# Reordering vector sums, weight splits and loads in a one-core adaLN attention and gated MLP kernel

## The chip, the cores and the metric

The kernel runs on one core of one Trainium2 chip. The metric is the device time of one execution in microseconds (us). An engine is called by its name in the profile: PE (TensorE matmuls), PEld (its weight loads), DVE (VectorE), ACT (ScalarE), POOL (GpSimd), SP (the engine that issues most loads). Each of them takes its instructions strictly in the order in which the program wrote them.

## The reference

What is computed is a transformer block on 2048 tokens of width 576, in float32:

```python
mod = silu(c) @ w_mod                         # six rows sa, ca, ga, sb, cb, gb
h = layernorm(x) * (1 + ca) + sa
q = (h @ wq) as 32 heads of 128;  k, v = last 512 cached keys, 16 heads, each used by 2 query heads
o = softmax(q @ k.T * 128 ** -0.5) @ v
x = x + ga * (o @ wo)
h = layernorm(x) * (1 + cb) + sb
x = x + gb * ((relu(h @ W_gate) * (h @ W_up)) @ W_down)     # inner width 4608
```

## The kernel before, in words

**Precision.** Matmul operands are pairs: a rounded high part (`hi`) and the rest, the low part (`lo` = value - hi). A product takes three matmuls: hi·hi, lo·hi, hi·lo. The high part is a copy on ACT, the low part a subtraction on POOL (`split`, L175 to 177, for weights).

**Attention.** The work is cut into 128 *units*. A unit is one query head and one block of 512 queries, against 512 keys. Units 0 to 87 go through KV heads 0 to 10 with all four query blocks (8 units a head). Units 88 to 107 do heads 11 to 15 for query blocks 0 and 1, units 108 to 127 the same heads for blocks 2 and 3, with 4 units a head. In unit u, PE does in this order: scores (`s_half`, 12 matmuls of 128x512), the query projection for unit u+1 (`qproj`, 14 matmuls), one small matmul that sends maxima and sums across partitions (`spread`, tile `qm`, L474), a quarter of an output projection (`piece`, 12 matmuls of 128x288), half of the product with the values of unit u-1 (`pv_half`, 6 matmuls), the other half, and a second quarter of an output projection.

The vector work of unit u hangs on this chain. DVE takes the maxima of the two score halves (L451), prepares them (L459, L460), sums the probabilities of unit u-1 over the partitions (`sum_pre`, L466, which reads `ks`), and then PE can do `spread`. After it DVE transposes the maxima (L489, L479, L504), subtracts them from the scores (L521, two instructions), and ACT does the exponentials (L523) and the high parts `hi` (L510). Then follow on DVE: `sum_bc` (L484, tile `rb`), `q_lo` (L430, the low part of the next queries), the first half of the probability sum (`ksum_op(u, 0)`, L536, which reads the first half of the exponentials), and `o_mul` (L556). POOL makes the low parts `lo` of the probabilities (`lo_half`, L530, one instruction for each half), the second half of the probability sum (`ksum_op(u, 1)`, L539, two instructions) and the low part of an attention output (`o_lo`, L564). In the program POOL's order is `lo` half 0, the sum, `lo` half 1. ACT also copies the output projection's PSUM result into `acc` (L584) and, where the next quarter allows it, puts `acc` into PSUM ahead of that quarter as a seed (L608).

**The order of side work** is written out by hand: `step(name, t, fn)` queues a function at time t, where unit u covers t = 10u to 10u + 9, and `run(u, k)` issues what is due at ten places in a unit. Place 0 lies ahead of the scores, 1 behind them, 2 behind the projection, 4 ahead of the exponentials, 5 between the two exponentials, 6 and 7 behind them, 8 ahead of `hi` of half 1, and 9 behind everything. Side work of this kind is:

- Weights for the next head (`prep`, `weights`, L1125): a load into one of two `raw` buffers on SP, for the output weights a multiplication with the gate row on DVE (*gate*, L217, tile `roga`), and a split on ACT and POOL (L176, L177). `gap` says how many quarter-units ahead of the split the load is written. "Parked" weights (`parks`) of heads 12 to 15 are prepared early and kept in HBM.
- `lay` (L1183): copies in HBM that bring the MLP weights into another layout, one every half unit, units 12 to 79, on SP.
- `prep_mod`: rows of `w_mod`, loads on SP and one multiply-add on DVE each (L128), every five units from unit 10.
- `w_later` (L823): the first MLP step needs seven combinations of weight blocks (`WTERMS`: P1, P2, P4 have one term, P7 and P5 two, P6 three, P3 four), in two halves each, 14 items in all. An item loads its terms from HBM, adds them on POOL (`comb`, L840), rounds on ACT (L849), subtracts on POOL (L850, L852) and stores both parts to HBM. The stores go out on ACT's queue (`flush_stores`). Before, they run in units 26 to 87, in `wp` weight buffers (tile `wx`).
- Behind unit 107 the second layer norm of blocks 0 and 1 (`norm_steps("b0")`, `("b1")`): statistics, normalising on ACT (`nm`), transposes on PE through the single PSUM buffer `psW` (`tr`, tile `ltb`, L317), scale and shift on ACT and DVE (`af`), stores. Then `h0_load`, `h0_cut`, `h0_comb` make the combined inputs of the MLP's first step.

**MLP.** 36 steps of seven products each (2 halves of the tokens, 18 blocks of the inner width), PE nearly alone at the end.

Of the kernel before, what the change touches and what calls it, by code (L numbers as in the profile page):

```python
# [7 lines left out]
F32 = mybir.dt.float32  # L8
F32R = mybir.dt.float32r
# [5 lines left out]
P = 128  # L15
# [18 lines left out]
def kernel(  # L34
# [614 lines left out]
    dkeep = [dr.tile([P, 2, D], F32R, name=f"dk{f}") for f in range(NFT)]  # L649
    stores = []  # L650

    def flush_stores():
        while stores:
            dst, src = stores.pop(0)
            nc.scalar.dma_start(dst.bitcast(F32), src.bitcast(F32))

# [163 lines left out]
    WTERMS = {"P1": "+00", "P2": "+01", "P6": "+10+11-00", "P7": "+00-10", "P5": "+10+11", "P4": "+11",  # L820
              "P3": "+01-10-11+00"}

    def w_later(s, xx, tag):  # L823
        st = {}
        eng = nc.gpsimd
        terms = terms_of(s, WTERMS)

        def get(dst, i, j):
            nc.sync.dma_start(dst, wlay[i, j, :, xx, :])

        def begin():
            w = wp.tile([P, 1280], F32, tag=tag, name=f"wx_{s}_{xx}")
            for k, x in enumerate("abh"):
                st[x] = w[:, 384 * k:384 * k + 384]
            for x, term in zip("ab", terms):
                get(st[x], *term[1:])

        def comb(i):
            x, y = st["a"], st["b"]
            eng.tensor_tensor(x, x, y, op=ALU.add if terms[i][0] == "+" else ALU.subtract)  # L840
            if i + 1 < len(terms):
                get(st["b"], *terms[i + 1][1:])
            else:
                cut()

        def cut():
            a = st["a"]
            hi = st["h"].bitcast(F32R)
            nc.scalar.copy(hi, a)  # L849
            nc.gpsimd.tensor_sub(hi[0:32, 256:], a[0:32, 256:], hi[0:32, 256:].bitcast(F32))  # L850
            lo = st["b"][:, :256].bitcast(F32R)
            nc.gpsimd.tensor_sub(lo, a[:, :256], hi[:, :256].bitcast(F32))  # L852
            stores.append((wkeep[0, s][:, xx, 0:3, :].rearrange("p t n -> p (t n)"), hi))
            stores.append((wkeep[0, s][:, xx, 3:5, :].rearrange("p t n -> p (t n)"), lo))

        return [begin] + ([cut] if len(terms) == 1 else [lambda i=i: comb(i) for i in range(1, len(terms))])
# [241 lines left out]
    for t in range(5):  # L1098
# [8 lines left out]
               (49, 46, 49), (("m", "aav", "vvv"), ("w", "vvv", "vvv"), ("w", "aav")))  # L1107
    H = 10 * UNITS.index((HKV - 1, 1, HQ - 1))
    norm_steps("b0", 0, "b", None, None, (H + 16, H + 20, H + 26, H + 29), H + 30,
               (H + 34, H + 36, H + 44, H + 46), (H + 48, H + 58, H + 68), (H + 49, H + 59, H + 69), www)  # L1110
    norm_steps("b1", 1, "b", None, None, (H + 34, H + 37, H + 40, H + 47), H + 48,
               (H + 54, H + 56, H + 64, H + 66), (H + 78, H + 88, H + 98), (H + 79, H + 89, H + 99), www)
    po = prep_out(wos, 0, wo, "ga")
    step("wo0.l", 19, po[0])
    step("wo0.g", 20, po[1])
# [9 lines left out]
    def weights(g, d):  # L1125

        h = 2 * g
        return [(("q", h), d["q"], prep5(d["q"], h, wq, "wA")), (("k", g), d["k"], prep_kv(d["k"], g, 0)),
                (("q", h + 1), d["q"], prep5(d["q"], h + 1, wq, "wA")),
                (("v", g), d["v"], prep_kv(d["v"], g, 1)), (("o", h), d["o"], prep_out(d["o"], h, wo, "ga")),  # L1130
                (("o", h + 1), d["o"], prep_out(d["o"], h + 1, wo, "ga"))]
# [6 lines left out]
    for i in range(1, len(VIS)):  # L1138
        g, qbs = VIS[i]
        B = 10 * UNITS.index((g, qbs[0], 2 * g))  # L1140
        if g in early or g in seen:
            for key, t in zip((("q", 2 * g), ("k", g), ("q", 2 * g + 1), ("v", g), ("o", 2 * g),
                               ("o", 2 * g + 1)), (-30, -20, -14, 0) + ((-4, -4) if i > first + 1 else (6, 34))):
                step("again", B + t, again, key, live[key[0]], key[1],
                     key[0] == "o" and key[1] % 2 and i > first and (i - first) % 2 == 0)
        else:
            for (key, d, pr), t in zip(weights(g, live), (-30, -20, -14, 0, 20, 34)):
                prep(key[0] + str(key[1]), B + t, pr, 3)
                if any(v[0] == g for v in VIS[i + 1:]):
                    sk(B + t + 12, key, d, key[1])  # L1150
        seen.add(g)
    WL = {i: [] for i in range(1, first)}
    longs = [(s, xx) for s in ("P3", "P6") for xx in range(2)]
    shorts = [(s, xx) for s in ("P1", "P2", "P7", "P5", "P4") for xx in range(2)]
    for i in range(1, first):
        B = 80 * i
        for c, t in (("q", 10), ("kv", 26), ("o", 44)):
            if parks[c]:
                key, d, pr = parks[c].pop(0)
                prep("park", B + t, pr, 3)  # L1160
                sk(B + t + 9, key, d, key[1])
        todo = []
        if i > 2:
            if longs or shorts:
                todo.append(((longs or shorts).pop(0), "wA", (24, 30, 36, 40)))
            if shorts:
                todo.append((shorts.pop(0), "wB", (40, 46)))
        for (s, xx), tag, ts in todo:
            fns = w_later(s, xx, tag)
            for fn, t in zip(fns, ts):  # L1170
                step("w.l", B + t, fn)
            step("w.st", B + ts[len(fns) - 1] + 5, flush_stores)
    assert not any(parks.values()) and not longs and not shorts
    for i in range(15):
        prep(f"m{3 + i // 5}.{i % 5}", 104 + 50 * i, prep_mod(3 + i // 5, i % 5))
    step("m3.col", 310, setd(mods, "b0", lambda: mod_col(3, 0.0)()))
# [71 lines left out]

    def then(fn):
        def go():  # L1250
            flush_stores()
            fn()
        return go

    t0 = H + 70
    for t in range(3):
        step("h0.l", t0, h0_load, 0, 0, t)
        step("h0.l", t0, h0_load, 1, 0, t)
    cuts = [("B11", (0, 0), t) for t in range(3)] + [("B21", (1, 0), t) for t in range(3)]
    for n, c in enumerate(cuts):  # L1260
        step("h0.c", t0 + 4 + 4 * n, then(lambda c=c: h0_cut(*c)))
    t0 = H + 100
    seq = []
    for t in range(3):
        step("h0.l", t0 + 4 * t, h0_load, 1, 1, t)
# [43 lines left out]
    run(-1, 9)  # L1309
    for u in range(NU):  # L1310
        run(u, 0)
        if u > 1:
            o_hi(u - 2)
            o_lo(u - 2)
        s_half(u, 0)
        s_half(u, 1)
        max_pre(u)
        if u:
            sum_pre(u - 1)
        run(u, 1)  # L1320
        if u + 1 < NU:
            qproj(u + 1, 0, 14)
        run(u, 2)
        spread(u)
        max_bc(u)
        if u + 1 < NU:
            q_hi(u + 1)
        run(u, 3)
        if 10 * u + 3 in at:
            piece(at[10 * u + 3])  # L1330
        run(u, 4)
        if u:
            pv_half(u - 1, 0)
        flush(pend_act)
        exp_half(u, 0)
        flush()
        run(u, 5)
        exp_half(u, 1)
        lo_half(u, 0)
        if u:  # L1340
            sum_bc(u - 1)
        if u + 1 < NU:
            q_lo(u + 1)
        run(u, 6)
        if u:
            pv_half(u - 1, 1)
        if 10 * u + 6 in at:
            piece(at[10 * u + 6])
        ksum_op(u, 0)
        run(u, 7)  # L1350
        if u:
            o_mul(u - 1)
        flush()
        run(u, 8)
        hi_half(u, 1)
        flush(pend_act)
        ksum_op(u, 1)
        lo_half(u, 1)
        run(u, 9)
    for u in range(NU, NU + 8):  # L1360
# [55 lines left out]
```

## Time and profile before

| what | value |
|---|---|
| runs | 3150.45, 3148.22, 3150.13 us; median 3150.13 |
| profiled execution | 3152.37 us, of which 3150.3 us lie between its first and last instruction (the span) |
| PE busy | 2939.7 us, 93% of the span |
| DVE, ACT, POOL busy | 2131.5, 1361.2 and 1859.4 us |
| mean granted TensorE clock | 0.982 |
| attention (scores from 35.1 to 1760.1 us) | PE waits here and there, all engines busy |
| MLP after it | the same code in both kernels |

In the rows of the profile, `out<-in` names what an instruction writes and reads, without buffer numbers. "Idle before" is the time in which the engine had nothing running ahead of that instruction, with the engine or transfer that ended it.

### The profile page before, as it was taken

How to read it: one execution, taken by the hardware profiler on the slowest of the kernel's cores; microseconds unless marked ns; L12 is line 12 of the kernel's file. 1: busy time of each engine (PE TensorE's matmuls, PEld its weight loads, DVE VectorE, ACT ScalarE, POOL GpSimd, SP SyncE). 2: the span in 40 equal slices, each digit the busy share in tenths (PEclk: the TensorE clock that was granted, in tenths of full speed). 3: DMA queues.
4: the chain of work that ended last, by engine and by line, in shares of the span. 5: the costliest groups of instructions: out<-in, count | busy, mean ns of one | idle time of the engine just before them, and what ended most of it. 6: DMA issues, size and time to landing. Idle time of an engine off the chain costs nothing. (4 is left out here: it accounts for less than half of the span.)

```text
span 3150.3 us, 41269 instructions
## 1 busy us (share of the span) xinstructions
PE 2939.7 (93%) x15414; PEld 2535.5 (80%) x15414; DVE 2131.5 (68%) x2925; ACT 1361.2 (43%) x1885; POOL 1859.4 (59%) x1294
## 2 busy tenths in 40 slices
PE   6799989988999999999888989999999999999999
PEld 5688877877887888888777777878778888888888
DVE  7888877777878887778778555556667544444444
ACT  5566655655666666665555333232323211111110
POOL 5688877787888777767678555556666411111111
PEclk9999999999999999999999999999999999999999
DMA  3122122223223112212244465556777954444453
GB/s 142 31 63 67 64 99 93 100 91 105 80 78 108 36 36 72 91 69 80 86 166 152 159 217 194 209 200 231 263 268 254 335 184 171 164 164 157 167 175 112
DMA packets 173447, 435.82 MB, mean 138 GB/s; under 512 B 16128, under 2 KB 62976, under 8 KB 173248
## 3 DMA queue, kind: packets, MB, share of 16 engines
q1 hardware_dynamic: 131344, 291.36, 28.1%
q10 hardware_dynamic: 41904, 141.84, 11.6%
q8 instruction: 122, 2.00, 0.3%
q14 instruction: 77, 0.63, 0.1%
HBM read 283.71 MB, written 177.73 MB: 146 GB/s over the span
## 5 line engine op out<-in xcount | busy, mean ns | idle before, releaser
L530 POOL TENSOR_TENSOR lo<-p,hi 128x1024 fp32r<-128x1024 f32 x256 | 623.2, 2435 | 314.4 <-ACT hi L510 281.1
L575 PE MATMUL md<-wogb,hhi 128*128 128x288 f32 x2304 | 480.7, 301 | 52.7 <-ACT lflh L900 32.1
L915 PE MATMUL gu<-hop_T,wop 128*128 128x512 f32 (+1 forms) x2016 | 502.4, 394 | 1.2 <-DMA wop<-wk_P 1.2
L586 DVE TENSOR_TENSOR acc<-md,acc 128x576 f32<-128x576 f32 x288 | 217.4, 755 | 422.3 <-PE md L575 422.3
L575 PEld LDWEIGHTS md<-wogb,hhi 128*128 128x128 f32 x2304 | 392.5, 192 | 83.4 <-ACT lflh L900 37.3
L915 PEld LDWEIGHTS gu<-hop_T,wop 128*128 128x128 f32 (+1 forms) x2016 | 370.6, 189 | 69.8 <-DMA wop<-wk_P 1.6
L451 DVE TRANSPOSE_TENSOR_REDUCE t<-s 128x32 f32<-128x1024 f32 x256 | 314.0, 1239 | 131.7 <-PE s L448 122.3
L915 PE MATMUL gu<-hop_B,wop 128*128 128x512 f32 (+1 forms) x1512 | 380.3, 394 | 4.1 <-DMA wop<-wk_P 2.7
L539 POOL TENSOR_TENSOR ks<-ks,p 128x512 f32<-128x512 f32 x256 | 341.3, 1333 | 18.9 <-DVE ks L536 6.5
L575 PE MATMUL md<-wogb,hlo 128*128 128x288 f32 x1152 | 345.8, 300 | 2.3 <-POOL hlo L931 2.3
L931 POOL TENSOR_TENSOR hlo<-r,hhi 128x512 fp32r<-128x512 f32 x72 | 98.7, 1371 | 409.2 <-issue 242.3
L915 PEld LDWEIGHTS gu<-hop_B,wop 128*128 128x128 f32 (+1 forms) x1512 | 280.6, 190 | 60.6 <-DMA wop<-wk_P 3.2
L374 PE MATMUL qps<-hTa,wA 128*128 128x512 f32 x1288 | 311.8, 393 | 8.7 <-ACT lfa L356 4.9
L575 PE MATMUL wo<-woga,ohi 128*128 128x288 f32 x1472 | 313.6, 306 | 5.0 <-ACT wo L608 3.5
L374 PEld LDWEIGHTS qps<-hTa,wA 128*128 128x128 f32 x1288 | 244.1, 190 | 61.8 <-ACT lfa L356 5.3
L521 DVE TENSOR_TENSOR p<-s,mb 128x1024 f32<-128x1024 f32 x242 | 285.5, 1217 | 3.5
L510 ACT CAST hi<-p 128x1024 fp32r<-128x1024 f32 x256 | 269.1, 1051 | 6.8
L523 ACT ACTIVATE p<-p 128x1024 f32<-128x1024 f32 x242 | 255.7, 1056 | 16.9 <-DVE p L521 10.5
L575 PEld LDWEIGHTS wo<-woga,ohi 128*128 128x128 f32 x1472 | 244.0, 193 | 15.4 <-ACT wo L608 5.2
L930 ACT CAST hhi<-r 128x512 fp32r<-128x512 f32 x72 | 44.7, 621 | 432.7 <-DVE r L940 379.5
L575 PEld LDWEIGHTS md<-wogb,hlo 128*128 128x128 f32 x1152 | 221.8, 193 | 3.0 <-POOL hlo L931 3.0
L575 PE MATMUL wo<-woga,olo 128*128 128x288 f32 x736 | 220.3, 299 | 0.0
(198 smaller groups left out, 5803.0 us busy)
## 6 DMA issues: line engine op xcount, KB each, us to landing
wop<-wk_P SPq DMA_DIRECT2D x133, 640.0 KB
wk_P<-wop ACTq DMA_DIRECT2D x119, 640.0 KB
wr<-wlay SPq DMA_DIRECT2D x68, 384.0 KB
dk<-wogb ACTq DMA_DIRECT2D x36, 576.0 KB
wogb<-dk SPq DMA_DIRECT2D x36, 576.0 KB
againq<-akq SPq DMA_DIRECT2D x18, 640.0 KB
rogb<-wd SPq DMA_DIRECT2D x36, 288.0 KB
rwA<-wq SPq DMA_DIRECT2D x32, 320.0 KB
```

Source lines behind the costliest of these rows:

```text
L374: return [lambda i=i, a=a, b=b: nc.tensor.matmul(ps, a, b, start=(i == 0), stop=(i == n - 1)) for i, (a, b) in enumerate(ops)]
L451: nc.vector.tensor_reduce(t4[u][:, 2 * h:2 * h + 2, :].rearrange("p k b -> p (k b)"), t.rearrange("p k (b j) -> p (k b) j", j=32), axis=AX ...
L510: nc.scalar.copy(hi_[u, h], pt[u, h])
L521: nc.vector.tensor_tensor(p, t, bc[u][:, None, :].to_broadcast([P, 2, 512]), op=ALU.subtract)
L523: nc.scalar.activation(p, p, AF.Exp, bias=0.0, scale=1.0)
L530: nc.gpsimd.tensor_sub(lo_[u, h], pt[u, h], hi_[u, h].bitcast(F32))
L539: nc.gpsimd.tensor_tensor(ks_[u], ks_[u], p[:, j, :], op=ALU.add)
L575: nc.tensor.matmul(ps[:, half, :H2], a[:, sl], w[b][:, cs], start=(n == 0 and seed is None), stop=(n == 5), skip_group_check=seed is not None)
L586: nc.vector.tensor_tensor(av, ps[:, :, :H2], av, op=ALU.add)
L915: nc.tensor.matmul(ps, a, c, start=s not in ("P2", "P3") and i == 0, stop=i == len(ops) - 1, skip_group_check=True)
L930: nc.scalar.copy(hi, r)
L931: nc.gpsimd.tensor_sub(lo, r, hi.bitcast(F32))
```

## The change

It has five parts, all in the order of the program; no arithmetic is changed. Where the diff writes `H`, it is 1070.

1. **Probability sums first.** `ksum_op(u, 0)` and `ksum_op(u, 1)` are written directly behind the second exponential, ahead of both `lo_half` calls. On POOL the sum now stands ahead of both low parts; on DVE L536 stands ahead of `sum_bc` and `q_lo`.
2. **Odd units' output split later.** `o_hi` and `o_lo` of odd units move from the start of the unit to behind `pv_half(u - 1, 0)`.
3. **Weight loads and splits spaced anew.** `gap` 3 becomes 4 (6 for the last), the first output weights' split moves from place 20 to 10 of a head's 80, the parked ones from 10, 26, 44 to 16, 24, 44 with gaps 5, 5, 6.
4. **`w_later` moved and rebuilt.** All 14 items go from units 26 to 87 to t = 952 to 1142 (units 95 to 115). They use two small tiles `wa`, `wb` (the high part overwrites `wb`, the low part `wa`) instead of one large one: the first seven items in `xm` buffers (three of them, shared with `ks`), the others in `hT` buffers, which are free once unit 107's projection is done. `flush_stores(2)` in the second group and in `h0_cut`'s steps leaves the two newest stores for a later call.
5. **Second norm of blocks 0 and 1.** Transposes go from place 8 of a unit to place 1 of the next but two (`H + 48` to `H + 51`), that is behind the scores, the normalising from places 4 and 6 to place 9, and the `h0` steps go four places later.

```diff
-    def flush_stores():
-        while stores:
+    def flush_stores(left=0):
+        while len(stores) > left:
...
         def begin():
-            w = wp.tile([P, 1280], F32, tag=tag, name=f"wx_{s}_{xx}")
-            for k, x in enumerate("abh"):
-                st[x] = w[:, 384 * k:384 * k + 384]
+            for x in "ab":
+                st[x] = pool.tile([P, w], F32, tag=tag, name=f"w{x}_{s}_{xx}")[:, :384]
...
-            hi = st["h"].bitcast(F32R)
+            hi = st["b"].bitcast(F32R)
...
-            lo = st["b"][:, :256].bitcast(F32R)
+            lo = a[:, :256].bitcast(F32R)
...
     norm_steps("b0", 0, "b", None, None, (H + 16, H + 20, H + 26, H + 29), H + 30,
-               (H + 34, H + 36, H + 44, H + 46), (H + 48, H + 58, H + 68), (H + 49, H + 59, H + 69), www)
+               (H + 39, H + 39, H + 49, H + 49), (H + 51, H + 61, H + 71), (H + 51, H + 61, H + 71), www)
...
-            for (key, d, pr), t in zip(weights(g, live), (-30, -20, -14, 0, 20, 34)):
-                prep(key[0] + str(key[1]), B + t, pr, 3)
+            for (key, d, pr), t in zip(weights(g, live), (-30, -20, -14, 0, 10, 34)):
+                prep(key[0] + str(key[1]), B + t, pr, 6 if t == 34 else 4)
...
-        for c, t in (("q", 10), ("kv", 26), ("o", 44)):
-            if parks[c]:
+        for c, t, gap, a in (("q", 16, 5, 0), ("kv", 24, 5, 1), ("o", 44, 6, 2)):
+            if parks[c] and i > a:
...
-        if i > 2:
-            if longs or shorts:
-                todo.append(((longs or shorts).pop(0), "wA", (24, 30, 36, 40)))
-            if shorts:
-                todo.append((shorts.pop(0), "wB", (40, 46)))
...
+    t = 952
+    items = [(s, xx) for s in ("P1", "P2", "P4", "P7", "P5", "P6", "P3") for xx in range(2)]
+    for n, (s, xx) in enumerate(items):
+        here = n < 7
+        for fn in w_later(s, xx, (xp, "xm", 640) if here else (hp, "hT", 512)):
+            step("w.l", t, fn if here else then(fn))
+            t += 5 if here else 4
+        if here:
+            step("w.e", t + 3, flush_stores)
+            t = t + 5 if n < 6 else 1062
+    step("w.e", t + 6, flush_stores)
...
-        if u > 1:
+        if u > 1 and u % 2 == 0:
             o_hi(u - 2)
             o_lo(u - 2)
...
             pv_half(u - 1, 0)
+        if u > 1 and u % 2:
+            o_hi(u - 2)
+            o_lo(u - 2)
         flush(pend_act)
         exp_half(u, 0)
         flush()
         run(u, 5)
         exp_half(u, 1)
-        lo_half(u, 0)
+        ksum_op(u, 0)
+        ksum_op(u, 1)
         if u:
             sum_bc(u - 1)
...
-        ksum_op(u, 0)
...
-        ksum_op(u, 1)
+        lo_half(u, 0)
         lo_half(u, 1)
```

POOL in units 60 and 61, before (`ks` is the probability sum, `lo` a low part, `wx` a `w_later` item, `wA` and `kv` weight splits):

```order
L530 TENSOR_TENSOR lo_0_8432<-p_0_8424,hi_0_8427 128x1024
L840 TENSOR_TENSOR wx_P_1_8341<-wx_P_1_8341 128x384
L850 TENSOR_TENSOR wx_P_1_8341<-wx_P_1_8341 32x128
L852 TENSOR_TENSOR wx_P_1_8341<-wx_P_1_8341 128x256
L539 TENSOR_TENSOR ks_8461<-ks_8461,p_1_8429 128x512 x2
L530 TENSOR_TENSOR lo_1_8471<-p_1_8429,hi_1_8464 128x1024
L177 TENSOR_TENSOR wA_8473<-rwA_8407,wA_8473 128x640
L564 TENSOR_TENSOR olo_8479<-rb_8434,ohi_8477 128x512
```

The same place now:

```order
L539 TENSOR_TENSOR ks_8321<-ks_8321,p_1_8318 128x512 x2
L530 TENSOR_TENSOR lo_0_8354<-p_0_8313,hi_0_8316 128x1024
L530 TENSOR_TENSOR lo_1_8356<-p_1_8318,hi_1_8349 128x1024
L177 TENSOR_TENSOR wA_8358<-rwA_8232,wA_8358 128x640
L564 TENSOR_TENSOR olo_8433<-rb_8325,ohi_8431 128x512
```

The sum no longer stands behind a low part and, here, a `wx` item.

DVE in unit 61, before (`p` is the subtraction ahead of the exponential, `t` with scores behind it the next unit's maxima):

```order
L521 TENSOR_TENSOR p_0_8555<-s_0_8481,mb_8525 128x1024
L521 TENSOR_TENSOR p_1_8560<-s_1_8490,mb_8525 128x1024
L484 STREAM_TRANSPOSE rb_8565<-ri_8523 128x512
L430 SCALAR_TENSOR_TENSOR qlo_8567<-qps_8505,qhi_8527 128x512
L536 TENSOR_TENSOR ks_8588<-p_0_8555 128x512
L556 TENSOR_TENSOR rb_8565<-pv_8545,rb_8565 128x512
L451 TENSOR_REDUCE t_62_8617<-s_0_8610 128x32
```

The same place now:

```order
L521 TENSOR_TENSOR p_0_8438<-s_0_8364,mb_8406 128x1024
L521 TENSOR_TENSOR p_1_8443<-s_1_8373,mb_8406 128x1024
L536 TENSOR_TENSOR ks_8446<-p_0_8438 128x512
L484 STREAM_TRANSPOSE rb_8450<-ri_8404 128x512
L430 SCALAR_TENSOR_TENSOR qlo_8452<-qps_8386,qhi_8408 128x512
L556 TENSOR_TENSOR rb_8450<-pv_8424,rb_8450 128x512
L451 TENSOR_REDUCE t_62_8500<-s_0_8493 128x32
```

`ks` reads the finished exponential, and `rb` and `qlo` now stand behind it.

ACT from the second exponential of unit 106 to the first of unit 107, before:

```order
L523 ACTIVATE p_1_14079<-p_1_14079 128x1024
L510 CAST hi_1_14111<-p_1_14079 128x1024
L584 COPY acc_131<-wo_2_14072 128x576
L608 COPY wo_3_14114<-acc_132 128x2x288
L560 CAST ohi_14120<-rb_14084 128x512
L426 ACTIVATE qhi_14168<-qps_14146 128x512
L584 COPY acc_132<-wo_3_14114 128x576
L608 COPY wo_0_14190<-acc_125 128x2x288
L523 ACTIVATE p_0_14192<-p_0_14192 128x1024
```

The same place now (`wb` is the rounding copy of a `w_later` item, which waits for POOL's `comb`):

```order
L523 ACTIVATE p_1_14015<-p_1_14015 128x1024
L849 CAST wb_P_1_13976<-wa_P_1_13975 128x384
L510 CAST hi_1_14051<-p_1_14015 128x1024
L584 COPY acc_131<-wo_2_14008 128x576
L608 COPY wo_3_14054<-acc_132 128x2x288
L426 ACTIVATE qhi_14108<-qps_14086 128x512
L849 CAST wb_P_0_14061<-wa_P_0_14060 128x384
L560 CAST ohi_14133<-rb_14022 128x512
L584 COPY acc_132<-wo_3_14054 128x576
L608 COPY wo_0_14138<-acc_125 128x2x288
L523 ACTIVATE p_0_14140<-p_0_14140 128x1024
```

Two rounding copies have come in, one ahead of `hi` of half 1, one ahead of the next unit's first exponential, and `ohi` of the odd unit stands behind `qhi`.

More of the change, by code (lines that the diff above doesn't have):

```diff
@@ L821, with w_later @@
               "P3": "+01-10-11+00"}
-    def w_later(s, xx, tag):
+    def w_later(s, xx, where):
+        pool, tag, w = where
         st = {}
@@ L1109 @@
     norm_steps("b0", 0, "b", None, None, (H + 16, H + 20, H + 26, H + 29), H + 30,
-               (H + 34, H + 36, H + 44, H + 46), (H + 48, H + 58, H + 68), (H + 49, H + 59, H + 69), www)
+               (H + 39, H + 39, H + 49, H + 49), (H + 51, H + 61, H + 71), (H + 51, H + 61, H + 71), www)
     norm_steps("b1", 1, "b", None, None, (H + 34, H + 37, H + 40, H + 47), H + 48,
-               (H + 54, H + 56, H + 64, H + 66), (H + 78, H + 88, H + 98), (H + 79, H + 89, H + 99), www)
+               (H + 59, H + 59, H + 69, H + 69), (H + 81, H + 91, H + 101), (H + 81, H + 91, H + 101), www)
     po = prep_out(wos, 0, wo, "ga")
@@ L1151 @@
         seen.add(g)
-    WL = {i: [] for i in range(1, first)}
-    longs = [(s, xx) for s in ("P3", "P6") for xx in range(2)]
-    shorts = [(s, xx) for s in ("P1", "P2", "P7", "P5", "P4") for xx in range(2)]
     for i in range(1, first):
         B = 80 * i
-        for c, t in (("q", 10), ("kv", 26), ("o", 44)):
-            if parks[c]:
+        for c, t, gap, a in (("q", 16, 5, 0), ("kv", 24, 5, 1), ("o", 44, 6, 2)):
+            if parks[c] and i > a:
                 key, d, pr = parks[c].pop(0)
-                prep("park", B + t, pr, 3)
+                prep("park", B + t, pr, gap)
                 sk(B + t + 9, key, d, key[1])
-        todo = []
-        if i > 2:
-            if longs or shorts:
-                todo.append(((longs or shorts).pop(0), "wA", (24, 30, 36, 40)))
-            if shorts:
-                todo.append((shorts.pop(0), "wB", (40, 46)))
[L1168 to L1173, printed above, removed]
+    assert not any(parks.values())
     for i in range(15):
@@ L1250, in go @@
         def go():
-            flush_stores()
+            flush_stores(2)
             fn()
         return go
-    t0 = H + 70
+    t = 952
[9 more added lines that the diff above has]
+    step("w.e", t + 6, flush_stores)
+    t0 = H + 74
     for t in range(3):
@@ L1261 @@
         step("h0.c", t0 + 4 + 4 * n, then(lambda c=c: h0_cut(*c)))
-    t0 = H + 100
+    t0 = H + 104
     seq = []
```

## The prediction

> **What bounds the kernel now.** I read the stretches first, counting PE's `spread` matmuls (line L474, two records a unit) in each. The columns are the stretch in us, its length, PE busy and count, PEld the same, granted clock, DMA share, GB/s.
>
> ```profile
> 133.00:374.20 241.20, 7.46 (x38) 6.35 (x39) 0.99 0.19 60
> 374.20:1137.50 763.30, 24.41 (x112) 18.87 (x113) 0.97 0.26 86
> 1137.50:1323.50 186.00, 6.02 (x30) 5.04 (x31) 1.00 0.20 66
> 1323.50:1481.00 157.50, 4.51 (x26) 4.98 (x27) 1.00 0.22 76
> 1481.00:1618.00 137.00, 3.54 (x19) 3.19 (x20) 0.98 0.33 112
> 1618.00:1763.00 145.00, 4.37 (x20) 2.85 (x19) 0.99 0.51 170
> ```
>
> In the fourth stretch (units 95 to 107) 13 units take 157.5 us, 12.1 each: PE never waits there, and no side work runs. That is the floor of a unit. The others hold 19, 56, 15, 9 and 10 units and take 11.3, 85.7, 4.5, 28.1 and 24.0 us more than 12.1 a unit. So 125 of these 154 us lie where the change takes something away, most of it in units 24 to 79, where `w_later` runs now.
>
> Next, who PE waits for: first in 374 to 1137 us, then (three rows) in 1481 to 1618, then in 1618 to 1763. The columns are us in total, times, longest.
>
> ```profile
> PE qm L474 <- DVE t L466: 47.4, 30, 6.6
> PE ltb L317 <- ACT acc L584: 6.7, 6, 2.8
> PE wo L575 <- ACT wo L608: 6.5, 7, 1.6
> PE qm L474 <- DVE t L466: 3.3, 2, 2.4
> PE qm L474 <- DVE t L466: 9.2, 7, 3.6
> ```
>
> `spread` waits for the sum over partitions. What makes that late stands in DVE's groups of 133 to 1323 us:
>
> ```profile
> L217 DVE TENSOR_TENSOR roga<-roga,mrow 128x576 f32<-128x576 f32 x30 | 75.6, 2520 | 28.5 <-DMA roga<-wo 28.5
> L466 DVE TRANSPOSE_TENSOR_REDUCE t<-ks 128x16 f32<-128x512 f32 x90 | 63.7, 708 | 38.5 <-POOL ks L539 36.9
> L536 DVE TENSOR_TENSOR ks<-p 128x512 f32<-128x512 f32 x90 | 62.4, 693 | 14.5 <-ACT p L523 14.5
> L128 DVE SCALAR_TENSOR_TENSOR macc<-wm,sT,macc 128x576 f32<-128x576 f32 x12 | 20.8, 1735 | 1.9 <-DMA wm<-wmod 1.9
> ```
>
> There are two causes: POOL's half of the probability sum (36.9 us of waiting), and gates whose weights have not landed (28.5 us, five times). The long ones cost more than they last. This is one, the wait ahead of unit 28, with a matmul behind it and the same matmul in an undisturbed unit:
>
> ```profile
> 426.18 2.40 DVE L217 TENSOR_TENSOR roga<-roga,mrow 128x576 f32<-128x576 f32 x1 [6.33 <-DMA roga<-wo]
> 432.11 0.71 PE L474 MATMUL qm<-t,quad 128*128 128x80 f32 x2 [6.59 <-DVE t L466]
> 433.18 0.44 PE L575 MATMUL wo<-woga,olo 128*128 128x288 f32 x1
> 1366.35 0.30 PE L575 MATMUL wo<-againo,olo 128*128 128x288 f32 x1
> ```
>
> The wait is 6.59 us, and the matmul then takes 0.44 instead of 0.30 us; the stretch's granted clock is 0.97 and not 1.00. So 85.7 us of excess stand against 47.4 us of `spread` waits. [...]
>
> **The sum ahead of the low parts.** An undisturbed unit (spread at 1360.3 us): DVE, ACT, POOL, the first score matmul that needs `qlo`, and the first matmul that needs the second low part:
>
> ```profile
> 1361.72 2.35 DVE L521 TENSOR_TENSOR p<-s,mb 128x1024 f32<-128x1024 f32 x2
> 1363.99 0.70 DVE L484 STREAM_TRANSPOSE rb<-ri 128x512 f32<-128x512 f32 x1
> 1364.62 0.65 DVE L430 SCALAR_TENSOR_TENSOR qlo<-qps,qhi 128x512 fp32r<-128x512 f32 x1
> 1365.19 0.67 DVE L536 TENSOR_TENSOR ks<-p 128x512 f32<-128x512 f32 x1
> 1363.66 1.05 ACT L523 ACTIVATE p<-p 128x1024 f32<-128x1024 f32 x1
> 1365.70 1.06 ACT L523 ACTIVATE p<-p 128x1024 f32<-128x1024 f32 x1
> 1365.88 2.41 POOL L530 TENSOR_TENSOR lo<-p,hi 128x1024 fp32r<-128x1024 f32 x1 [3.02 <-ACT hi L510]
> 1368.24 2.67 POOL L539 TENSOR_TENSOR ks<-ks,p 128x512 f32<-128x512 f32 x2
> 1370.86 2.39 POOL L530 TENSOR_TENSOR lo<-p,hi 128x1024 fp32r<-128x1024 f32 x1
> 1366.94 0.40 PE L448 MATMUL s<-qlo,againk 128*128 128x512 f32 x1
> 1376.08 0.39 PE L550 MATMUL pv<-lo,againv 128*128 128x512 f32 x1
> ```
>
> POOL's sum now ends at 1370.91. Written first, it starts when the second exponential ends (1366.76) and is done at 1369.4, 1.5 us earlier. A weight split or a `wx` item in front of it then no longer reaches `spread`, so the 36.9 us of waiting go. What is late next is the low parts: they end at 1369.4 + 4.8 = 1374.2 instead of 1373.25. PE needs the second one at 1376.1 (last row), so this is hidden with 1.9 us to spare.
>
> On DVE the sum's first half now waits for the first exponential. It starts at 1364.7 (1363.66 + 1.05) where `rb` started at 1363.99. At the rows' spacing of 0.6 us `qlo` starts two places later, at 1365.9, and ends at 1366.6 instead of 1365.3; PE needs it at 1366.94. The cover is 0.3 us. It holds in a plain unit. It does not in a unit with a multiply-add of `w_mod` ahead of the exponentials (1.74 us): there `qlo` comes at about 1367.7 to 1368.3, and I put 1 us on each of 15 such units.
>
> Odd units' `ohi` no longer stands ahead of `qhi`; ACT's exponential comes no later by it, and I cost it at nothing, since the copy that follows waits for PE anyway.
>
> **Gates.** Whether a gate delays the score maxima behind it hangs on what POOL is doing: a gate, POOL's instruction beside it, and a gate with POOL idle:
>
> ```profile
> 189.16 2.94 DVE L217 TENSOR_TENSOR roga<-roga,mrow 128x576 f32<-128x576 f32 x1
> 189.08 2.41 POOL L530 TENSOR_TENSOR lo<-p,hi 128x1024 fp32r<-128x1024 f32 x1 [2.35 <-ACT hi L510]
> 82.57 0.74 DVE L217 TENSOR_TENSOR roga<-roga,mrow 128x576 f32<-128x576 f32 x1
> ```
>
> The gate ends at 192.1, 0.6 us behind the low part's end at 191.5. After the change it starts about 0.75 us later in its unit, but POOL is in one of the two short sum instructions (1.33 us each), so it ends no later than now: 0.2 us for each of 30. If it took 2.94 us all the same, each would cost 0.75 us more, 22 us in all; that is a rival below. [...]
>
> **Loads and `w_later` taken away, units 5 to 94.** The five late gates stand where an item of three or four terms begins in the same place as the weight load. Those loads go, and the weight loads are written up to a unit earlier, so I let the 28.5 us go. Of 85.7 us there remain 11 multiply-adds at 1 us, 21 gates at 0.2, some 3 us of other waits, and the two column sums, which the change leaves alone:
>
> ```profile
> L165 PE MATMUL mps<-ones,macc 128*128 128x1 f32 x20 | 3.6, 289 | 4.4 <-DVE macc L162 2.6 <-DVE qlo L430 1.8
> ```
>
> These are 8.0 us, so 26 remain and 60 are gained. Of 11.3 us in the first stretch 4.5 remain (three multiply-adds, gates), of 4.5 in the third 3. The sum is 60 + 7 + 1.5 = **68 us gained**.
>
> **`w_later` put back, units 95 to 115.** Its instructions, ACT's wait for POOL in all (us, times), and the longest of these:
>
> ```profile
> L840 POOL TENSOR_TENSOR wx_P<-wx_P x14: 1012/1016/1506, 414.5 to 990.5; 128x384 f32<-128x384 f32 x14
> L849 ACT CAST wx_P<-wx_P x14: 493/511/517, 429.5 to 1094.1; 128x384 fp32r<-128x384 f32 x14
> L850 POOL TENSOR_TENSOR wx_P<-wx_P x14: 445/451/455, 430.0 to 1095.6; 32x128 fp32r<-32x128 f32 x14
> L852 POOL TENSOR_TENSOR wx_P<-wx_P x14: 716/727/738, 430.5 to 1096.1; 128x256 fp32r<-128x256 f32 x14
> POOL wx_P L840: 37.0, 8
> 429.46 0.51 ACT L849 CAST wx_P<-wx_P 128x384 fp32r<-128x384 f32 x1 [6.60 <-POOL wx_P L840]
> ```
>
> POOL's work is 14 x (1.02 + 0.45 + 0.73) = 31 us over 20 units, 1.5 a unit beside the 7.5 of 12.1 us that low parts and sum take above, and would fit. The order is the trouble. A rounding copy waits for POOL's last `comb`, eight items have one, and now (37.0 us in 8, 4.6 each) most of these waits stand at the start of a unit, where ACT idles. In the new order those of P5, the first of P6 and the first of P3 stand ahead of a unit's exponential. POOL reaches `comb` only behind the low parts of the unit before (about 1.8 us behind spread) and its last term arrives only after the `comb` before it. I put the copy's end 2 to 5 us behind where the exponential begins now, and `qlo` and the seed late by as much: 4 + 3 + 6.5 + 3.5. The last P3 copy holds up `hi` and both low parts, 4, and the other three cost 1.5 each. That is **25.5 us given back**, between 0 (all hidden) and 8 x 6.6 = 53 (the last row for each). For the six one-term items, whose loads share buffers with `ks`, I add 1.5: **27 us**.
>
> **Norm and `h0`.** The transposes are now covered by the 12 score matmuls, and the seed behind them by the projection's 14. Of the 6.7 + 6.5 us of waits I let 9 go, because some stand ahead of the first transpose. The `h0` steps fall on other places of a unit, which I cost at nothing, 5 us either way; POOL's earlier sum takes 2 of the 9.2 us in units 117 to 126. **11 us gained.**
>
> The sum is 68 - 27 + 11 = 52 us. The profiled execution took 3152.4 us, so 3100.4; the median of the runs lies 2.2 us below it, so **3098 us**. The MLP's code is the same.
>
> **The rivals.**
>
> *More is given back* (chance 0.20). The eight items cost the full 53 us: 3098 + 27 = 3125, from 3117 to 3140. For it: POOL, ACT and SP are in order, so one late term stops all three. Against: the stretch starts with no wait at all.
>
> *Gates still wait 2.9 us* (0.08): 3098 + 22 = 3120.
>
> *The late loads stay* (0.05), since HBM copies on SP's queue are the cause and not the items: 28.5 us, some 2 us of slower matmuls behind each (an estimate from 85.7 against 47.4), and 6 us of other waits in these units, about 45 us: 3143. The change would then not do what its second part says, and the result is at the edge of no change.
>
> *More is gained* (0.13): items hidden (12 instead of 27) and the multiply-adds' 15 us too: 3098 - 15 - 13 = 3070.
>
> *Slower* (0.06): the 0.3 us of cover ahead of `qlo` is not there. If the first exponential ends 0.3 us later than in the unit shown, every unit loses; at 0.8 us in 120 units 96 us come back, 3194. For it: L536 waited 14.5 us for exponentials already where it stood two instructions later. Against: in the unit shown it had 0.3 us to spare.
>
> **The numbers.** The forecast, 3075 to 3117, has 0.48. About 0.2% (6.3 us) is what a measurement of this kernel can tell from no change. Faster by more than that takes in the forecast, the first, second and fourth rival and part of the third: 0.89; within it 0.05; slower 0.06. The range from 3066 to 3130 leaves out the slower case, the late loads, and the ends of the two wide rivals, 2 in 10.
>
> **What would show it.** In the changed profile units 24 to 79 should take about 703 us, 12.6 each, at granted clock 1.00, with L466's wait for POOL gone and no row of L217 waiting for a load. Beside L448 a wait for `qlo` should stand only in units with a multiply-add. ACT's `wb` copy should wait for POOL in units 104 to 113 by 25 to 40 us, with PE waiting for `qlo` and for seeds there. The `ltb` waits should be gone. I am wrong if units 24 to 79 still take over 13 us, or if units 95 to 103, which lose nothing by my account, take over 12.3.

## The result, and the profile after

The changed kernel takes 3130.53 us (median of 4 runs, 3127.97 to 3133.55) against 3149.18 us for the kernel before in the same comparison: a ratio of 0.9944, 95% interval 0.9927 to 0.9961. It is faster, by 18.6 us, where 52 were forecast. The profiled execution took 3133.55 us, with a span of 3131.8.

These are the prediction's six stretches, cut at the same units. The columns are the stretch, its length, PE's `spread` matmuls (busy and count), granted clock, DMA share, GB/s.

```profile
143.00:379.50 236.50, 6.84 (x39) 1.00 0.16 50
379.50:1108.70 729.20, 20.27 (x112) 0.97 0.24 79
1108.70:1293.20 184.50, 5.36 (x30) 1.00 0.22 73
1293.20:1456.90 163.70, 4.51 (x26) 0.99 0.33 110
1456.90:1600.40 143.50, 3.64 (x19) 0.93 0.39 130
1600.40:1748.50 148.10, 4.09 (x20) 0.95 0.49 160
```

| part of the span | forecast, us | measured, us |
|---|---|---|
| up to unit 5 | 0 | +10.0 |
| units 5 to 23 | -7 | -4.7 |
| units 24 to 79 | -60 | -34.1 |
| units 80 to 94 | -1.5 | -1.5 |
| units 95 to 126 | -11 + 27 | +15.8 |
| behind unit 126 (MLP) | 0 | -4.0 |

So 26 us are missing in units 24 to 79, and 10 at the start, a stretch for which the prediction has no term. Units 24 to 79 take 13.02 us each at a granted clock of 0.97, where 12.6 at 1.00 were expected and more than 13 was named as the sign of being wrong. The last row is the spread between executions: the MLP's code is the same in all kernels of this study, and that part took 1381 to 1389 us in their profiles.

DVE's waits in units 24 to 79 (total, times, longest) say what kind of wait is left:

```profile
DVE macc L128 <- DMA wm<-wmod: 17.8, 3, 6.8
DVE macc L126 <- DMA wm<-wmod: 6.5, 1, 6.5
DVE roga L217 <- DMA roga<-wo: 0.9, 1, 0.9
```

The gates (28.5 us before) now have their weights, and L466's wait for POOL is gone, as forecast. But four multiply-adds of `prep_mod` wait for their row of `w_mod`. Before, one did, for 1.9 us. This is the one in unit 30: SP's queue, DVE, and some of PE's next score matmuls (start, duration):

```profile
449.70 0.58 SPq L1169 DMA_DIRECT2D wlay<-wu  x1
450.33 5.47 SPq L136 DMA_DIRECT2D wm<-wmod  x1
455.85 6.05 SPq L1169 DMA_DIRECT2D wlay<-wg  x2
461.83 0.82 DVE L128 SCALAR_TENSOR_TENSOR macc<-wm,sT,macc 128x576 f32<-128x576 f32 x1 [6.83 <-DMA wm<-wmod]
469.64 0.63 PE L447 MATMUL s<-qhi,kv 128*128 128x512 f32 x1
470.07 0.63 PE L448 MATMUL s<-qlo,kv 128*128 128x512 f32 x1
472.90 0.40 PE L446 MATMUL s<-qhi,kv 128*128 128x512 f32 x1
473.13 0.39 PE L447 MATMUL s<-qhi,kv 128*128 128x512 f32 x1
```

The load's issue, right behind an HBM copy, takes 5.47 us, and the row lands 6 us behind its end. Units 30, 35, 45 and 50, where these four waits stand, take 23.1, 20.7, 19.2 and 19.4 us: 82.4 together.

Behind unit 95 the profile is for the most part the forecast's (window 1293 to 1600 us):

```profile
ACT wb_P L849 <- POOL wa_P L840: 39.4, 8, 7.2
PE wo L575 <- ACT wo L608: 14.4, 10, 4.1
PE ltb L317 <- ACT acc L584: 2.1, 1, 2.1
```

ACT's rounding copies wait 39.4 us for POOL (25 to 40 forecast), PE pays with waits for seeds, though hardly for `qlo` (0.6 us), and `ltb`'s waits have shrunk from 6.7 to 2.1 us, where the forecast had them gone.

At the start, the stretch from 35 us to unit 5's `spread`, before and then after, and PE's new wait in it (all columns PE, PEld, DVE, ACT, POOL, clock, DMA share, GB/s):

```profile
35.00:132.90 97.90, 72.91 (x314) 56.29 (x312) 83.87 (x137) 47.73 (x68) 58.29 (x40) 0.91 0.09 31
```

```profile
35.00:143.00 108.00, 82.01 (x325) 64.03 (x323) 84.90 (x137) 47.93 (x69) 58.22 (x40) 0.81 0.08 28
PE lta L317 <- DVE rb L556: 5.5, 1, 5.5
```

**A correction.** The section on the chip says that each engine takes its instructions in the written order. For SP this is wrong: line 50 fixes that order for PE, DVE, ACT and POOL alone. The trace shows it: the HBM copies, written for units 12 to 79, begin at 34.4 us, while the `spread` of unit 12 comes at 230.5 us. POOL and DVE do run in the written order where the prediction shows them (1361 to 1374 us of before).

```profile
L1169 SPq DMA_DIRECT2D wlay<-wg x68: 579/758/5827, 34.4 to 1041.5; - x68
```

### The profile page after: what moved, and what is told of

It reads as the page before. It is cut to its first block, busy times and chain, and to the rows that moved or that the text cites. A ratio compares the mean times of both kernels' runs of the same rounds, so it can differ in the third digit from the quotient of the medians.

```text
span 3131.8 us, 41177 instructions
## 1 busy us (share of the span) xinstructions
PE 2949.8 (94%) x15414; PEld 2544.4 (81%) x15414; DVE 2102.8 (67%) x2925; ACT 1369.8 (44%) x1885; POOL 1848.4 (59%) x1294
## 3 DMA queue, kind: packets, MB, share of 16 engines
q1 hardware_dynamic: 131344, 291.36, 28.5%
## 5 line engine op out<-in xcount | busy, mean ns | idle before, releaser
L530 POOL TENSOR_TENSOR lo<-p,hi 128x1024 fp32r<-128x1024 f32 x256 | 612.6, 2415 | 1.2 <-ACT hi L510 0.9
L931 POOL TENSOR_TENSOR hlo<-r,hhi 128x512 fp32r<-128x512 f32 x72 | 98.9, 1374 | 408.9 <-issue 242.4
L575 PE MATMUL wo<-woga,ohi 128*128 128x288 f32 x1472 | 305.9, 300 | 2.3 <-DVE lfa L354 1.6
L426 ACT ACTIVATE qhi<-qps 128x512 fp32r<-128x512 f32 x128 | 76.4, 597 | 350.5 <-PE qps L374 340.5
```

The costliest lines, as they stand in the source:

```text
L426: nc.scalar.activation(qhi[u], qst[u][0], AF.Copy, bias=0.0, scale=SCALE)
L530: nc.gpsimd.tensor_sub(lo_[u, h], pt[u, h], hi_[u, h].bitcast(F32))
L575: nc.tensor.matmul(ps[:, half, :H2], a[:, sl], w[b][:, cs], start=(n == 0 and seed is None), stop=(n == 5), skip_group_check=seed is not None)
L931: nc.gpsimd.tensor_sub(lo, r, hi.bitcast(F32))
```

## The experiments

The first question was what holds up the rows of `w_mod`; then what each part is worth alone; then the start and the rounding copies. "Units 24 to 79" is the time between the `spread`s of units 24 and 80: 763.3 us before, 729.2 after. Ratios are to the kernel before, with 95% intervals.

### 1. The rows of `w_mod` loaded earlier

```diff
-        prep(f"m{3 + i // 5}.{i % 5}", 104 + 50 * i, prep_mod(3 + i // 5, i % 5))
+        prep(f"m{3 + i // 5}.{i % 5}", 104 + 50 * i, prep_mod(3 + i // 5, i % 5), 4)
```

> The kernel after, with the loads of the w_mod rows (tile wm) written four quarter-units ahead of their multiply-add instead of two; nothing else is edited. Theory Q (the queue): the five long waits of after (units 30, 35, 45, 50, 55, together 101.4 us) come from wm loads that have too short a lead on SP, whose queue stands about 5.2 us behind each HBM copy. With twice the lead the five units take about 12.8 us each like the other units with a multiply-add: 37 us less, 3094 us, ratio to before about 0.982. Rival S (the queue is simply full, so some load is late whatever the order): the waits move to gates (L217) or weight splits, 3120 to 3131 us. Rival M (the multiply-add itself costs it, not its load): the five units stay, 3130 us.

3104.24 us, 0.9852 (0.983 to 0.9875). Units 24 to 79:

```profile
377.20:1078.50 701.30, 20.44 (x112) 1.00 0.26 82
```

28 us of the stretch go. Units 30, 35, 45 and 50 take 53.2 instead of 82.4 us, and gates wait 2.9 us. Theory Q holds and S and M fall, but I had counted one unit too many: unit 55 stays at 18.8 us. Its multiply-add never waited. It has a column sum behind it (L165), and it is long in every kernel of this list.

### 2. HBM copies described by rows

```diff
-            return [(wlay[f:f + 2, j, :, xx, 0:256], src[f:f + 2, :, 256 * j:256 * j + 256])
+            return [(wlay[f:f + 2, j, :, xx, 0:256].rearrange("f p n -> p f n"),
+                     src[f:f + 2, :, 256 * j:256 * j + 256].rearrange("f p n -> p f n"))
```

The copies of `rest` are changed in the same way.

> The kernel after, with the HBM copies that bring the MLP weights into another layout (lay) described with the 128 (or 32) rows as the outermost dimension instead of the 2 (or 9) blocks; the same bytes go to the same places. Theory Q: a copy keeps only some 2 of the 16 DMA engines busy (DMA share 0.1 while it runs at 48 GB/s), and every load behind it waits for those two. Spread over all 16 a copy takes about 1 us, SP no longer has issues of over 2 us in units 24 to 79, no wm or gate load is late, and the time is 3085 to 3097 us (ratio 0.980 to 0.983). Rival B (the loads wait for their buffers, which POOL's splits release, and the copies are not to blame): five units still wait, over 3118 us. Rival S (the bytes are the limit): the copies take as long as before, 3130 us.

3103.95 us, 0.9853 (0.9833 to 0.9873); units 24 to 79 take 701.8 us. First a stretch of after in which nothing but a copy moves data, then one of this kernel full of copies (in the second, all engines), and the issue of the row for unit 30:

```profile
457.60:461.40 3.80, 2.35 (x16) 1.00 0.15 53
```

```profile
90.00:120.00 30.00, 22.48 (x104) 18.12 (x104) 24.21 (x47) 16.91 (x26) 12.92 (x11) 0.94 1.01 316
440.73 0.38 SPq L136 DMA_DIRECT2D wm<-wmod  x1
```

A copy had 0.15 of 16 engines, some two of them (an estimate: 0.15 x 16 = 2.4), and 53 GB/s. In the stretch full of copies described by rows, the share was 1.01 at 316 GB/s, and the same issue that took 5.47 us takes 0.38. The experiment changes two things at once, though: the rate rises from 53 to 316 GB/s, and SP's new order has the copies all between 34 and 203 us. It shows that they are what holds up the loads. That the higher rate alone would do is not shown.

### 3. Old gaps: the change without its third part

```diff
-            ... (-30, -20, -14, 0, 10, 34)):
-                prep(key[0] + str(key[1]), B + t, pr, 6 if t == 34 else 4)
+            ... (-30, -20, -14, 0, 20, 34)):
+                prep(key[0] + str(key[1]), B + t, pr, 3)
...
-        for c, t, gap, a in (("q", 16, 5, 0), ("kv", 24, 5, 1), ("o", 44, 6, 2)):
+        for c, t, gap, a in (("q", 10, 3, 0), ("kv", 26, 3, 0), ("o", 44, 3, 0)):
```

> The kernel after with its third part undone: weight loads three quarter-units ahead of their splits, the first output weights at place 20, the parked ones at 10, 26 and 44 as before. Theory Q: the spacing only decides which load is late. The wm loads come in time again and some gates (L217) wait 5 to 6 us again: 3115 to 3135 us. The prediction's step (the gates were late because w_later items stood in the same place): neither the gates nor the wm loads are late, about 3095 us. Rival: the old spacing is worse for the splits too, over 3140 us.

3099.6 us, 0.9836 (0.9815 to 0.9856). Theory Q missed here, since no gate became late again; the prediction's step is borne out:

```profile
378.00:1077.30 699.30, 19.60 (x113) 0.99 0.25 80
```

Without the third part the stretch gains 64.0 us, where the forecast had 60. So the new spacing itself costs 30 us. How it does can be seen ahead of unit 35's multiply-add. SP's queue in after, then in this kernel:

```profile
511.64 1.05 SPq L213 DMA_DIRECT2D roga<-wo  x1
512.74 6.47 SPq L1169 DMA_DIRECT2D wlay<-wg  x2
519.31 7.12 SPq L213 DMA_DIRECT2D roga<-wo  x1
526.53 0.37 SPq L136 DMA_DIRECT2D wm<-wmod  x1
```

```profile
508.30 0.34 SPq L213 DMA_DIRECT2D roga<-wo  x1
508.68 0.58 SPq L1169 DMA_DIRECT2D wlay<-wg  x1
509.37 1.57 SPq L136 DMA_DIRECT2D wm<-wmod  x1
510.98 0.73 SPq L1169 DMA_DIRECT2D wlay<-wu  x1
515.54 1.96 SPq L213 DMA_DIRECT2D roga<-wo  x1
```

In after the second `roga`, a parked weight with a lead of six quarters, stands ahead of `wm`, behind two copies. With a lead of three it comes behind `wm`.

### 4. The first two parts alone

The kernel before, with the sums first and the odd units' output split late (the diff of the change's section).

> The kernel before with the first two parts of the change alone: probability sums ahead of the low parts, odd units' output split behind the first half of the product with the values. Prediction's step: POOL's 36.9 us of waiting in units 5 to 94 go, and about 30 us come off: 3119 us, ratio 0.990; the five late gates stay. Rival (the sums were hidden behind loads, which set the pace): under 10 us come off, 3140 us or more. Rival (the cover ahead of qlo is lost): slower than 3150 us.

3151.94 us, 1.0009 (0.9997 to 1.002): nothing, and units 24 to 79 take 762.3 us. L466 no longer waits for POOL at all (26.5 us before in this stretch), yet the stretch keeps its length. PE's waits in it say where the time went, first for seeds in before, then in this kernel:

```profile
PE wo L575 <- ACT wo L608: 2.8, 3, 1.1
```

```profile
PE qm L474 <- DVE t L466: 30.4, 5, 8.9
PE wo L575 <- ACT wo L608: 6.9, 4, 3.0
PE wo L575 <- POOL olo L564: 6.8, 8, 1.3
```

PE waited 47.4 us for the sum before. The short ones of these waits fall from 22.3 to 2.2 us, but the four long ones, behind late gates, grow from 25.1 to 28.2, and PE's other waits grow from 9.7 to 23.3: for seeds, for the low part of an output (`olo`, not once before), for `qlo`. So most of what the sums save is waited for again at other places, and a smaller part at the late gates. Here are three late gates of this kernel, and then two of before:

```profile
426.35 0.93 DVE L217 TENSOR_TENSOR roga<-roga,mrow 128x576 f32<-128x576 f32 x1 [7.31 <-DMA roga<-wo]
539.89 0.87 DVE L217 TENSOR_TENSOR roga<-roga,mrow 128x576 f32<-128x576 f32 x1 [6.61 <-DMA roga<-wo]
763.12 4.29 DVE L217 TENSOR_TENSOR roga<-roga,mrow 128x576 f32<-128x576 f32 x1 [6.88 <-DMA wk_P<-wx_P]
```

```profile
541.75 1.59 DVE L217 TENSOR_TENSOR roga<-roga,mrow 128x576 f32<-128x576 f32 x1 [7.16 <-DMA roga<-wo]
761.89 1.51 DVE L217 TENSOR_TENSOR roga<-roga,mrow 128x576 f32<-128x576 f32 x1 [6.67 <-DMA roga<-wo]
```

With the 426.18 of the prediction, they start within 2 us of each other. A fourth starts 4.0 us earlier than before (647.35 against 651.33 us), but takes 6.28 us instead of 1.37. Both stretches begin at the same time (374.2 and 374.3 us); this kernel is 2.6 us ahead at unit 32, 3.4 at unit 40, behind by 0.9 at unit 44, after the next late gate, and by 5.9 at unit 60, and 1.1 ahead at unit 80. These three gates came at most 1.9 us earlier, so what was saved ahead of them beyond that was waited for there. That this accounts for the whole saving is not shown, and the 13.6 us of other waits speak against it.

### 5. The fourth part alone

The kernel before, with `w_later` rebuilt and moved as in the change.

> The kernel before with the change's fourth part alone: the w_later items moved from units 26 to 87 to units 95 to 115 and rebuilt; sums, spacing and norm as before. Theory P (in units 24 to 79 the loads set the pace as long as the items stand on SP and POOL; with the sums first alone nothing came off, 762.3 against 763.4 us there): without the items the gates come in time, units 24 to 79 take 715 to 735 us, some 20 us of short waits for POOL's sum remain, and 12 to 17 us are given back behind unit 95: 3115 to 3130 us. Rival A (the parts add up, so the sums are worth nothing here either): units 24 to 79 take about 700 us, 3095 to 3105 us. Rival B (the items were hidden, only their giving back shows): 3150 to 3170 us.

3125.26 us, 0.9911 (0.9895 to 0.9928). Units 24 to 79, and DVE's waits for the sum there:

```profile
374.30:1091.20 716.90, 22.32 (x112) 0.99 0.24 78
DVE t L466 <- POOL ks L539: 17.9, 16, 2.5
```

No gate waits any more, and 46 us of the stretch go; 18.5 are given back behind unit 95 (458.0 against 439.5 us). Theory P holds, though slightly more is given back than its 12 to 17 us. With experiments 3 and 4: the sums are worth 18 us in this stretch (716.9 to 699.3) with the items away and the loads on time, and 1 us with the items there and the loads late. Which of the two conditions counts is not shown: no run has the order of before with wide copies and the items in place.

### 6. The old order in units 0 to 4

On the kernel of experiment 3, parts 1 and 2 begin with unit 5:

```diff
-        ksum_op(u, 0)
-        ksum_op(u, 1)
+        if u >= 5:
+            ksum_op(u, 0)
+            ksum_op(u, 1)
+        else:
+            lo_half(u, 0)
```

The second low part, L536 and the odd units' output split go by the same condition.

> The kernel of old gaps with units 0 to 4 in the order of before (low part, sum, low part; odd units' output split at the start of the unit), all later units as in after. Theory O (the new order itself costs at the start, where the first exponential and the norm's copies are late and qlo now stands behind the sum): unit 5's spread comes at about 133 us instead of 142.5, and about 7 us come off, 3092 us. Rival G (the start is longer for another reason, as the granted clock of that execution or the weight loads): spread 5 stays between 138 and 143 us, and the time at 3099 us.

3092.59 us, 0.9805 (0.979 to 0.982). Unit 5's `spread` comes at 133.1 us:

```profile
35.00:133.10 98.10, 73.87 (x310) 0.88 0.09 29
```

Over all profiles, it stands at 132.8 to 134.1 us in the five with the old order at the start, and at 138.5 to 143.0 in the nine with the new one. Theory O holds. PE's wait of 5.5 us for `rb` is absent from this kernel's list of waits. How the loss of 6 to 10 us divides between that wait and the granted clock (0.81 to 0.89 against 0.88 to 0.91 where I looked) is settled only in part: two kernels with the same order there, experiments 3 and 7, reach unit 5 at 142.5 us with a clock of 0.81 and at 138.9 with 0.89, and the wait of 5.5 us is in both. So 3.6 us of it go with the clock.

### 7. The fifth part undone

On the kernel of experiment 3, with the times of `norm_steps` and `t0` of before.

> The kernel of old gaps with the fifth part undone: norm transposes, normalising and the h0 steps of blocks 0 and 1 at their places of before. Prediction's step: the fifth part is worth 11 us (9 of waits at ltb, 2 at the sums), so 3110 us, with waits of ltb for acc again in units 110 to 116. Rival (beside the w_later items it gives nothing, since ACT is late there for their sake): within 4 us of 3099.6.

3106.67 us, 0.9849 (0.9833 to 0.9866). Units 108 to 126 take 300.6 instead of 290.4 us, and PE's waits at `ltb` are back:

```profile
PE ltb L317 <- ACT acc L584: 4.8, 6, 0.9
```

The part is worth 7 us by the medians, which come from different comparisons and take in the start (unit 5 at 138.9 against 142.5 us), and 10 by the stretch. The forecast of 11 was slightly high.

### 8. The rounding copy a step later

On the kernel of experiment 3, an item's last step on POOL and the copy that needs it are parted:

```diff
-            else:
-                cut()
...
+        fns = w_later(s, xx, (xp, "xm", 640) if here else (hp, "hT", 512))
+        cut = [] if here else [fns.pop()]
...
+        for fn in cut:
+            step("w.l", t + 2, then(fn))
```

> The kernel of old gaps, in which the rounding copy of a w_later item of several terms is a step of its own, half a unit behind the last combination on POOL, so that ACT need not stand and wait for POOL. Prediction's step (25 us of the given back come from that wait; after shows 39.4 us of ACT waiting in 8): units 105 to 117 lose 10 to 20 us, 3080 to 3090 us. Rival W (POOL's work itself is what is late, wherever ACT waits): the waits move to the sums and low parts, and at most 4 us come off.

3081.58 us, 0.977 (0.9755 to 0.9785). ACT's wait for POOL in the kernel of experiment 3, and then in this one (L849 is L847 there), with units 95 to 107 and 108 to 116:

```profile
  ACT wb_P L849: 40.2, 8
```

```profile
  ACT wb_P L847: 2.9, 2
1260.10:1419.60 159.50, 4.50 (x26) 1.00 0.34 112
1419.60:1548.60 129.00, 3.32 (x18) 0.97 0.45 145
```

POOL does the same work, and the two stretches shrink by 3.5 and 13.0 us. The forecast priced this wait at 25.5 us; it is worth 17 in units 95 to 126 (453.4 to 436.4).

### 9. Only the leads undone

The kernel after, with 3 in place of the leads 4, 5 and 6, and the new times of the splits kept.

> The kernel after with only the leads of the weight loads undone (three quarter-units ahead of the split instead of four, five or six); the times of the splits stay as in after (first output weights at place 10, parked ones at 16, 24, 44). Theory L (a load written earlier takes its place on SP ahead of a wm load, waits there for a buffer and holds the wm load up): the wm loads are on time, units 24 to 79 take about 700 us, 3097 to 3104 us. Rival T (it is the new times of the splits that crowd the queue): some wm or gate loads are still 5 us late, units 24 to 79 take over 715 us, 3115 to 3131 us.

3106.32 us, 0.985 (0.9822 to 0.9879), units 24 to 79 take 702.7 us. Theory L holds: of the third part's 30 us in this stretch, the leads make 26.5. The median is 2 us above the band expected; the new times of the splits can account for no more than the 3.4 us that are left of the stretch. Whether the earlier loads hold up the others by waiting for a buffer, as the theory says, or by their place alone, no run separates.

### 10. The sums alone, with wide copies

The kernel of experiment 4 with the copies of experiment 2; the `w_later` items stay where they were.

> The kernel of the sums alone (before with the first two parts, which came out at no change) with the HBM copies described by rows, over 16 instead of 2 DMA engines; the w_later items stay in units 26 to 87. Theory C (the copies hold SP's queue, so the gates land at the same time however fast the units run): the gates land on time, units 24 to 79 take 705 to 725 us instead of 762, 3100 to 3115 us. Rival I (the items' own waits on SP, for buffers and stores, make the gates late): they stay late, units 24 to 79 over 745 us, 3130 us or more.

3120.85 us, 0.9901 (0.9876 to 0.9925). Units 24 to 79, DVE's wait for gates, and ACT's for the items:

```profile
376.10:1110.10 734.00, 19.37 (x112) 0.98 0.18 58
DVE roga L217 <- DMA roga<-wo: 0.4, 1, 0.4
ACT wx_P L850 <- POOL wx_P L841: 45.8, 8, 7.7
```

Neither band was met. The gates are on time with the items still there, as theory C has it, and 28 us of the stretch go. What remains over 700 us stands beside the items' rounding copies, which wait 45.8 us for POOL here as they do later in after. PE waits 28.1 us in the stretch, against 7.3 in experiment 3, most of it for the low part of an output (9.0), seeds (8.7) and `qlo` (7.4). So with the items in place the sums first bring new waits even when no gate is late; that the rounding copies make them is likely, not shown.

### 11 and 12. The findings together

Old gaps, the old order in units 0 to 4 and the later rounding copy; then the same with wide copies.

> Three findings together: after with the old gaps, the old order in units 0 to 4, and the rounding copies of the items a step later. If they are independent: 3099.6 - 7 - 18 = 3074.6 us; the start at 133 us, units 24 to 79 about 698, units 95 to 126 about 436 us. Rival (they overlap, since the rest of the start's loss returns as a wait for loads): 3080 us.

> The kernel before this one in the list (old gaps, old start, rounding later) with the wide HBM copies as well. Theory: with no load late any more there is nothing left for them to mend, within 3 us of 3075. Rival: units 30 and 55, still 16 to 18 us long, lose their rest by loads, and 5 to 8 us more come off. Rival: the copies, which now all run in the first 200 us, delay the first weight loads, 5 us or more slower than 3075.

3076.4 us, 0.9761 (0.9736 to 0.9787), and 3078.77 us, 0.977 (0.9746 to 0.9795). Unit 5 comes at 133.9 us and units 24 to 79 take 696.7 us in the first, so by the stretches the parts add up, but for units 95 to 126 (440.2 us, 436 expected). Both beat the change, by 52 to 54 us. The wide copies have nothing left to mend. Experiments 8, 11 and 12 cannot be told apart by their times; the first of the three is told apart from 11 by its profile alone (unit 5 at 141.5 us).

## Why the prediction was wrong

**The step that failed** is "the weight loads are written up to a unit earlier, so I let the 28.5 us go". It looked at the gates alone. They did come in time, in after and in experiments 3 and 5. But the loads written earlier took their place in SP's queue ahead of others (519.31 against 526.53 us in after, 515.54 against 509.37 in experiment 3), and I never followed whose place that was. Four rows of `w_mod`, with a lead of two quarters, came to stand behind weight loads and copies. They cost 82.4 - 54.9 = 27.5 us against the old gaps, of the 30 us that the third part loses. The prediction names no queue that the loads are moved past, and I took SP's order for the written one.

**Why the loads were late before** was argued as the items' doing, with copies on SP's queue as the rival (0.05), in the form that the late loads stay. The runs show that either takes them away: no items (experiment 5), or copies described by rows (10). The forecast's outcome held without the third part, and what it said of the cause was half of it.

**The sums.** The mechanism was right: POOL's wait is gone wherever they come first. That the 36.9 us come off by themselves was not: of the 26.5 us that fall on units 24 to 79 the sums alone bring nothing (4), and 18 with the items away and the loads on time (3 and 5). With the items in place the time is waited for again, mostly for seeds, outputs' low parts and `qlo`, which now come late, and in part at the late gates; the prediction followed only the low parts of the probabilities.

**The start** had no term: 6 to 10 us lost (6). The cover of 0.3 us ahead of `qlo` was examined in a unit of the steady state only. There it held: units 96 to 104 take 12.08 us each, as before, and the slower rival is refuted.

**The gates' rival** is refuted as well: gates take 1.58 us on average in units 5 to 94, where they took 2.52. The 0.2 us that the forecast counts for each gate was an estimate that no run shows; these averages are what the runs have in its place.

```profile
L217 DVE TENSOR_TENSOR roga<-roga,mrow 128x576 f32<-128x576 f32 x30 | 47.4, 1581 | 0.9 <-DMA roga<-wo 0.9
```

**Behind unit 95** the sum came out, 15.8 against 16 us, by luck, since its terms did not: 17 instead of 25.5 us for the rounding copies (8), and 10 instead of 11 for the norm (7, by the stretch). Experiment 7, which has the items but not the norm's part, takes 463.5 us in units 95 to 126, 24.0 more than before. So some 7 us beside the rounding copies were given back, where the prediction had 1.5; what they are is open.

Put together, the forecast of 3098 us is what the change without its third part takes: 3099.6 us. That is in part luck, since the start's loss of 9.5 us is in it, and is made up by 4 us more gained in units 24 to 79, 2 us less given back behind unit 95, and an MLP that was 4 us shorter in that execution.

Two slips in the prediction's numbers change nothing of this. The rival in which more is gained takes 13 us for the multiply-adds, where its words say 15. And the chance of 0.89 is the sum without any part of the third rival.

## What to carry to other kernels

An earlier load can change the order on a queue that others share: list what it now stands ahead of, and how much lead those loads had (here four of them were waited for 24.3 us in all, which cost 27.5). Time saved at one wait can come back at others: in experiment 4 PE's long waits behind late loads grew from 25.1 to 28.2 us, and its waits for other things, most of them for what now came later, from 9.7 to 23.3. So the sums were worth 18 us of units 24 to 79 with the loads on time and the items away, and 1 us with the loads late and the items there: test the parts alone and together. Where one engine copies, in a fixed order, what another has just been told to compute, try the copy a step later: it gave 17 us here (experiment 8).

## What the runs showed of the hardware

An HBM copy whose outer dimension is 2 ran at 53 GB/s with a DMA share of 0.15. At that rate 256 KB, the size of these copies, take 4.9 us (an estimate). In units 24 to 79 of after, 16 loads were issued on SP's queue right behind such a copy, within 0.5 us: 12 of the issues took 5.0 to 5.7 us, three 6.6 to 7.1, and one 1.7. Three more, right behind a copy of 144 KB, took 0.4 to 0.5. In a stretch full of copies with their rows outermost the share was 1.01 at 316 GB/s, and the three issues of SP from 440 to 453 us of experiment 2 took 0.33 to 0.38 us.

After a wait of 7 us, which ended at 466.91 us, PE's score matmuls came 0.43 us apart from 469.64 to 472.63, and then 0.23 (the rows of unit 30 above); the granted clock was 0.50 from 466.90 to 472.63 and 0.99 from there to 476.80. The slower stretch lasted 5.7 us from the end of the wait. The four waits for `w_mod` lasted 24.3 us and cost 27.5.
